# A block-sparse attention and mixture-of-experts kernel: three edits in how the attention copies, loads and scales

## The chip, the cores and the metric

The kernel runs on one core of one Trainium2 chip. The metric is the time of one execution on the device in microseconds (us). Engines are named as the profile names them: PE is TensorE (matrix products, and transposes as products with an identity), PEld its weight loads, DVE is VectorE, ACT is ScalarE, POOL is GpSimd, SP is SyncE, which here only issues transfers (DMAs). PSUM is the memory in banks into which PE writes its results.

## What is computed

Attention over 4 batches, 8 heads, 768 positions, 64 columns, with a mask by blocks of 32 positions; then every row of the result goes through two of eight experts.

```python
mask = np.abs(blk_i - blk_j) <= window                     # window = 1
mask = mask | (blk_i == 0) | (blk_j == 0) | (blk_i == n_blocks - 1) | (blk_j == n_blocks - 1)
for qb in range(n_blocks):
    for kb in sampled_blocks[qb]:                          # 3 blocks, drawn at random
        mask[qb * block:(qb + 1) * block, kb * block:(kb + 1) * block] = True
...
out = softmax(scale * q @ k.T where mask) @ v              # x, 3072 rows of 512
noisy = x @ w_gate + log1p(exp(x @ w_noise)) * noise       # the best two of 8 experts
out[row] = sum over its two experts e of weight[row, e] * relu(x[row] @ w1[e]) @ w2[e]
```

(The last three lines put a longer passage into short words; F, the hidden width, is 1024.)

## The kernel before

The attention comes first (0 to about 312 us of the profile), the experts after it. Only the attention is touched.

**Items.** A batch has six tiles t of 128 query rows, that is four blocks of 32, and each tile is worked in two head halves f: twelve items ("q", b, t, f). Four items more ("g", b, i, par) do the first and last block, which attend to everything. `steps` (L467) walks through all items as a pipeline. In step k it does, in this order of code: `turn` of item k (transpose its exponentials), `high` and `low` of item k-2 (its finished rows split into two fp16 parts, ACT L416 and POOL L423), `scores` of item k+2 (PE, L264), `soft` of it (DVE maximum L301, ACT exponentials L304), `cut` (DVE L346, zeroes a corner of the first and last tile), `global_av` (PE L382) and `av` of item k-1 (PE L359, with `norm` on DVE L366 to L369), and then the loads and preparations for later. Each engine runs its own instructions in that order and waits at semaphores for the others; the scores, the transposes and thus three steps share a ring of three PSUM tiles `ps` of two banks each.

**turn.** Eight transposes go into the two banks of the item's `ps`. DVE copies bank 0 out (L335, or L321 for g items) and ACT copies bank 1 (L333, L319) into `ptr` or `pgt`, from where `av` reads. `apart(it, bank, x)` declares that x doesn't depend on instructions that were noted for the other bank; the framework, which tracks a tile as a whole, then places no wait between the two. In the kernel before it is used for the transposes, not for ACT's copy.

**Rows of v.** A tile needs for each of its four blocks (three in the first and last tile) the three neighbouring blocks of v and three sampled ones. The neighbours lie ready in an array `vw`, 96 partitions by one block (j) by 2 KB; the sampled ("listed") rows are 64 KB transfers of their own (L232). `prefetch_v(b, t, half)` is called for half 0 in one step and for half 1 in the next; each call loads the neighbours of the half's two blocks (L227, 384 KB) and its six listed transfers. A tile has a buffer pair va, vb out of three; in the last batch out of two, so that a load there waits for the `av` of two tiles earlier.

**SP's queue.** SP issues the transfers one after another, in program order: v, `q` of a tile (L195), a piece of the next batch's keys `kk` (L172), stores, and from the last batch on the experts' weights `wraw` (L905) and zeroes for the output (L1334). An instruction issues only when the transfer eight before it has landed: the semaphores DMAHW0 to DMAHW7 take turns.

**Keys.** The next batch's keys come in six pieces of 256 KB, one an item, and `scale_k` (L184) multiplies a piece by 0.125 on POOL, i = 2t + f - 1 counting the items. `prefetch_k` (L204, L205 on POOL, L207 on ACT) then gathers a tile's keys out of `kk` into `kc`, which the scores read.

Of the kernel before, what the change touches and what calls it, by code (L numbers as in the profile page):

```python
# [16 lines left out]
AF = mybir.ActivationFunctionType  # L17
# [31 lines left out]
class Attention:  # L49
# [159 lines left out]
    def prefetch_v(self, b, t, half):  # L209
        nc, HD, J = self.nc, self.HD, self.NJ  # L210
        i = self.which(b, t)
        if half == 0:
            self.listed_rows[i] = []
        va, vb = self.va[i], self.vb[i]
        self.st["v", b, t] = va, vb
        js = self.real(t)
        first = t * J + js[0]
        if half == 0:
            self.unlisted = self.held_v.get(t)
            if self.unlisted is None:  # L220
                self.unlisted = self.numbers(self.mi[0:1, 3 * first:3 * (first + len(js))], mybir.EngineType.SP,
                                             self.NB * self.RB)
                if t in KEEP:
                    self.held_v[t] = self.unlisted
        js = [j for j in js if j // 2 == half]
        part = lambda x: x.rearrange("p (j c) -> p j c", j=J)[:, js[0]:js[-1] + 1]
        nc.sync.dma_start(va[0:96, js[0]:js[-1] + 1, 0:HD], part(self.vw[b, t]))  # L227
        rows = self.vx[b].rearrange("s c -> (s c)").bitcast(U8)
        for j in js:
            for n, d in enumerate((va[96:128, j], vb[0:32, j], vb[32:64, j])):  # L230
                at = self.unlisted[3 * (t * J + j - first) + n]
                x = nc.sync.dma_start(d[:, 0:HD].bitcast(U8), rows[bass.ds(at, self.RB)].rearrange("(p c) -> p c", p=32))  # L232
                self.listed_rows.setdefault(i, []).append(x)
                self.beside(x, self.weights.get(i, ()))
# [72 lines left out]
    def turn(self, it):  # L307
        nc = self.nc
        s = self.st.pop((it, "s"))
        if it[0] == "g":  # L310
            pg = self.st.pop((it, "p"))
            d = self.pgt[2 * it[2] + it[3]]
            for x in range(2):
                t = s[:, x].rearrange("p (c k) -> p c k", c=4)
                for c in range(4):
                    k = 96 * (4 * x + c)
                    self.apart(it, x, nc.tensor.transpose(t[0:96, c], pg[:, k:k + 96], self.ident))
                if x:
                    nc.scalar.activation(d[0:96, 4:8], t[0:96], AF.Copy)  # L319
                else:  # L320
                    read = nc.vector.tensor_copy(d[0:96, 0:4], t[0:96])  # L321
                    self.st[it, "read"].append((0, read))
            del self.st[it, "read"]
            return
        p = self.st.pop((it, "p"))
        d = self.st[it, "pt"] = self.pp.tile([P, 2, 2, 2, P], F32, name="ptr")
        for par in range(2):
            t = s[:, par].rearrange("p (e c k) -> p e c k", e=2, c=2)
            for e in (1, 0):
                for c in range(2):  # L330
                    self.apart(it, par, nc.tensor.transpose(t[:, e, c], p[:, 2 * e + par, P * c:P * c + P], self.ident))  # L331
            if par:
                nc.scalar.activation(d[:, par], t, AF.Copy)  # L333
            else:
                self.st[it, "read"].append((0, nc.vector.tensor_copy(d[:, par], t)))  # L335
        del self.st[it, "read"]
# [130 lines left out]
    def steps(self, router, done, background):  # L467
# [8 lines left out]
        for k in range(-2, n + 7):  # L476
# [48 lines left out]
            if new[0] == "q" and new[1] + 1 < B:  # L525
# [3 lines left out]
                if i == 2:  # L529
                    self.load_g(new[1] + 1)  # L530
                    self.load_ends(new[1] + 1)
                if 3 <= i <= 8:
                    self.scale_k(new[1] + 1, i - 3, 6, nc.gpsimd)
            if new[0] == "q" and new[3] == 1 and nk < len(tg):
                self.prefetch_k(*tg[nk])
                nk += 1
# [1041 lines left out]
```

## Time and profile before

| | |
|---|---|
| three runs | 857.63, 859.27, 862.04 us; median 859.27 us |
| profiled execution | 864.39 us, of which the span of the profile is 862.5 us |
| PE busy in the span | 792.3 us (92%) |
| DVE, ACT, POOL busy | 585.3, 401.4, 379.7 us |
| attention | 0 to about 312 us; last batch's part from about 236 us |
| experts | from about 320 us, PE busy throughout |

A row of a timeline shows the start, the duration, the engine, the line, the operation, what it writes and reads, how many instructions stand in the row, and in brackets how long the engine was idle just before and whose work ended that. "SPq" rows are issues by SP, several of them in one row with the short gaps between. The chain of waits follows the work that ended last back from the end; there a DMA row lasts from the issue to the landing that something waited for. "issue" is time for which the profile shows no reason.

### The profile page before, as it was taken

Reading aid. Unit: us, or ns where it says so; the run is one execution under the profiler, and the core shown is the slowest. Engines: PE = TensorE matmul, PEld = TensorE weight load, DVE = VectorE, ACT = ScalarE, POOL = GpSimd, SP = SyncE. Lnnn points to the kernel's source line nnn. Section 1 sums busy time; section 2 is a strip of 40 time slices with the busy share of each in tenths; the row PEclk is TensorE's granted clock in tenths of the full one; section 3 lists DMA queues with packets and bytes.
Section 4 is the critical chain, followed back from the end, with each engine's and each line's share of the span. In section 5 each row is a group of like instructions: output and inputs, shape, how many; then the busy total and the mean of one; then the engine's idle time right before and its main releaser. Section 6 shows DMA issues by size and latency. Waiting matters only on the chain.

```text
span 862.5 us, 24909 instructions
## 1 busy us (share of the span) xinstructions
PE 792.3 (92%) x9799; PEld 487.7 (57%) x9799; DVE 585.3 (68%) x1160; ACT 401.4 (47%) x736; POOL 379.7 (44%) x656
## 2 busy tenths in 40 slices
PE   7898889888877769999998999999999999999995
PEld 4676566565645647566586554554554554554552
DVE  6665697788787427762429698697697796796621
ACT  5868758848735325322113551542642633543500
POOL 5773587567554230130624526426335345323211
PEclk7999999999988859999999999999999999999998
DMA  7755786686669975650877839639539549533301
GB/s 229 218 177 169 213 233 187 199 242 188 226 189 266 224 178 162 192 186 22 219 161 140 241 110 235 189 101 234 172 112 230 170 128 216 164 98 104 97 31 50
DMA packets 119842, 148.87 MB, mean 173 GB/s; under 512 B 69515, under 2 KB 76300, under 8 KB 119714
## 3 DMA queue, kind: packets, MB, share of 16 engines
q1 hardware_dynamic: 107490, 109.22, 47.6%
q0 software_dynamic: 12224, 37.96, 14.0%
q8 instruction: 79, 1.29, 0.7%
q14 instruction: 49, 0.40, 0.2%
HBM read 107.28 MB, written 26.15 MB: 155 GB/s over the span
## 4 chain that ended last, share of the span: by engine, by line
PE 71%; DVE 11%; DMA 7%; ACT 5%; issue 3%; SPq 2%; POOL 1%; DVEq 0%; POOLq 0%; ACTq 0%
PE pc L1142 28%; PE pa L1095 11%; PE pd L1095 5%; PE po L359 5%; PE ps L264 4%; PE pa L1056 4%; PE pc L1095 3%; PE ps L331 3%; PE pd L1056 2%; PE pc L1151 2%; DMA va<-in_vx_dram 2%; DVE m L301 2%; DMA vb<-in_vx_dram 2%; DMA va<-in_vw_dram 2%; ACT p L304 2%
## 5 line engine op out<-in xcount | busy, mean ns | idle before, releaser
L1142 PE MATMUL pc<-w,hh 128*128 128x512 f16 x768 | 228.4, 379 | 0.0
L1175 POOL DMA_INDIRECT out_dram<-y,r_xT x46 | 64.2, 1395 | 220.3 <-DVE y L1174 181.6
L1142 PE MATMUL pc<-w,hl 128*128 128x512 f16 x384 | 145.5, 379 | 0.0
L1095 PEld LDWEIGHTS <-w 128*128 128x128 f16 x1008 | 99.2, 98 | 81.0 <-issue 6.2
L1142 PEld LDWEIGHTS <-hh 128*128 128x128 f16 x768 | 74.6, 98 | 86.4
L304 ACT ACTIVATE p<-ps,m 128x256 f32<-128x256 f32 x192 | 75.3, 476 | 24.6 <-DVE m L301 20.3
L204 POOL COPY kc<-kk 128x128 f32 x264 | 69.4, 300 | 23.0 <-PE ps L264 15.3
L359 PE MATMUL po<-va,ptr 128*32 128x68 f32 x1536 | 61.4, 236 | 17.2 <-DMA va<-in_vx_dram 10.2
L301 DVE TENSOR_REDUCE m<-ps 128x4 f32<-128x1024 f32 x48 | 58.6, 1221 | 22.6 <-PE ps L264 22.6
L998 POOL DMA_INDIRECT xg<-x_rows,r_xT x46 | 60.0, 1304 | 14.7 <-issue 14.7
L264 PE MATMUL ps<-kc,q 64*32 64x256 f32 x1536 | 57.0, 395 | 8.8 <-issue 3.8
L944 DVE SCALAR_TENSOR_TENSOR w<-wraw,w 128x1024 f16<-128x1024 f32 (+1 forms) x58 | 64.2, 1109 | 0.8 <-ACT w L940 0.8
L359 PE MATMUL po<-vb,ptr 128*32 128x68 f32 x1536 | 58.9, 233 | 4.8 <-issue 3.6
L1142 PEld LDWEIGHTS <-hl 128*128 128x128 f16 x384 | 37.6, 98 | 45.3
L1016 POOL DMA_INDIRECT pv<-out_dram,r_xT x44 | 49.0, 1113 | 28.2 <-issue 24.0
L1095 PE MATMUL pa<-tb,w 128*128 128x408 f16 x288 | 56.5, 340 | 3.3 <-ACT ta L1083 3.3
L359 PEld LDWEIGHTS po<-va,ptr 128*32 128x32 f32 x1536 | 42.8, 115 | 28.7 <-issue 8.4
L940 ACT ACTIVATE w<-wraw 128x1024 f16<-128x1024 f32 (+1 forms) x58 | 55.6, 959 | 6.6 <-DMA wraw<-in_moe_w_dram 6.6
L1174 DVE SCALAR_TENSOR_TENSOR y<-pc,r_xT,pv 128x512 f32<-128x512 f32 x37 | 27.7, 749 | 43.6 <-PE pc L1142 43.0
L1095 PE MATMUL pd<-tb,w 128*128 128x408 f16 x288 | 56.5, 336 | 0.0
L333 ACT ACTIVATE ptr<-ps 128x512 f32<-128x512 f32 x48 | 28.8, 600 | 57.6 <-DVE ptr L335 49.3
L1064 ACT ACTIVATE hh<-pa 128x408 f16<-128x408 f32 (+2 forms) x56 | 24.1, 443 | 65.6 <-PE pa L1056 53.2
(239 smaller groups left out, 1573.2 us busy)
## 6 DMA issues: line engine op xcount, KB each, us to landing
wraw<-in_moe_w_dram SPq DMA_DIRECT2D x64, 512.0 KB
va<-in_vw_dram SPq DMA_DIRECT2D x40, 384.0 KB
vb<-in_vx_dram SPq DMA_DIRECT2D x176, 64.0 KB
q<-in_qt_dram SPq DMA_DIRECT2D x24, 256.0 KB
va<-in_vx_dram SPq DMA_DIRECT2D x88, 64.0 KB
kk<-in_kt_dram SPq DMA_DIRECT2D x18, 256.0 KB
x_rows<-x SPq DMA_DIRECT2D x16, 256.0 KB
out_dram<-x SPq DMA_DIRECT2D x4, 768.0 KB
```

The lines of the kernel that those rows point to most:

```text
L204: nc.gpsimd.tensor_copy(kc[:, j, :, 3 + n], flat[:, bass.ds(self.listed(blk, n), P)].rearrange("p (n c) -> p n c", c=32))
L264: mm = lambda o, l, r: nc.tensor.matmul(o, l, r, start=True, stop=True, skip_group_check=True)
L301: nc.vector.tensor_reduce(m, s.rearrange("p a (e c) -> p a e c", e=2), axis=AX.X, op=ALU.max, negate=True)
L304: i = nc.scalar.activation(p[:, 2 * e + par], s[:, par, 256 * e:256 * e + 256], AF.Exp, bias=m[:, par, e:e + 1])
L359: nc.tensor.matmul(o[32 * j:32 * j + 32, h], d[:, h % 2, h // 2, x, 32 * j:32 * j + 32], self.values(v[:, self.slot(t, j)], 4 * f + h), st ...
L940: self.nc.scalar.activation(hi, t, AF.Copy, scale=WS)
L944: self.nc.vector.scalar_tensor_tensor(lo, t, WS, hi, op0=ALU.mult, op1=ALU.subtract)
L998: nc.gpsimd.indirect_dma_start(out=self.xg[0:m, c + self.place(u)], out_offset=None, in_=self.x_dram[0:nr], in_offset=bass.IndirectOffsetO ...
L1056: nc.tensor.matmul(ph[:, 0:m], w[:, wt, slot, kb % 2 * P:kb % 2 * P + P], r["xt"][:, kb, a, o:o + m], start=i == 0, stop=i == last)
L1095: nc.tensor.matmul(o, w[:, wt, slot, s * P:s * P + P], mv(s, a), start=i == 0 and p in tail, stop=i == 5, skip_group_check=True)
L1142: nc.tensor.matmul(py, h[:, f, o], w(f)[:, x], start=i == 0, stop=i == last)
L1175: d = nc.gpsimd.indirect_dma_start(out=self.out, out_offset=bass.IndirectOffsetOnAxis(ap=r["ix"][0:m, c:c + 1], axis=0), in_=y[0:m], in_of ...
```

## The change

Three edits, all in the class `Attention`.

```diff
+        if half == 0:
+            part = lambda x: x.rearrange("p (j c) -> p j c", j=J)[:, js[0]:js[-1] + 1]
+            nc.sync.dma_start(va[0:96, js[0]:js[-1] + 1, 0:HD], part(self.vw[b, t]))
         js = [j for j in js if j // 2 == half]
-        part = lambda x: x.rearrange("p (j c) -> p j c", j=J)[:, js[0]:js[-1] + 1]
-        nc.sync.dma_start(va[0:96, js[0]:js[-1] + 1, 0:HD], part(self.vw[b, t]))
...
-                    nc.scalar.activation(d[0:96, 4:8], t[0:96], AF.Copy)
+                    self.apart(it, 1, nc.scalar.activation(d[0:96, 4:8], t[0:96], AF.Copy))
...
-                nc.scalar.activation(d[:, par], t, AF.Copy)
+                self.apart(it, 1, nc.scalar.activation(d[:, par], t, AF.Copy))
...
-                if 3 <= i <= 8:
-                    self.scale_k(new[1] + 1, i - 3, 6, nc.gpsimd)
+                for x in ((0,), (1, 2), (3,), (4, 5))[i - 5] if 5 <= i <= 8 else ():
+                    self.scale_k(new[1] + 1, x, 6, nc.gpsimd)
```

(In the diff above the last loop is the program's own text as far as `scale_k`, whose argument is x in both.) Edit A makes ACT's copies of bank 1 independent of DVE's copies of bank 0. Edit B loads all neighbours of a tile with half 0, in one transfer of 768 KB (576 KB for the first and last tile); half 1 has only listed rows left. Edit C leaves i = 3 and 4 without a scale and does pieces 0; 1 and 2; 3; 4 and 5 at i = 5, 6, 7, 8.

What stands in the engines' queues, before and after. Line numbers after are larger by one from L228 on. "waits" names the semaphores: an engine's, or DMAHWn for the landing of a transfer. First ACT, an ordinary q item in the first batch: `turn`'s copy, the first fp16 part, four exponentials. Before:

```order
L333 ACTIVATE ptr<-ps 128x512 [waits DVE_49,PE_49]
L416 ACTIVATE x_955<-xr 128x2x128 [waits DMAHW2_49]
L304 ACTIVATE p<-ps,m 128x256 [waits DVE_49,Activation_49]
L304 ACTIVATE p<-ps,m 128x256 x3
L257 ACTIVATE vb_99<-ends_108 64x2x512
```

After:

```order
L334 ACTIVATE ptr<-ps 128x512 [waits PE_49,Activation_49]
L417 ACTIVATE x_949<-xr 128x2x128 [waits DMAHW2_49,DVE_49]
L305 ACTIVATE p<-ps,m 128x256 [waits DVE_49,Activation_49]
L305 ACTIVATE p<-ps,m 128x256 x3
L258 ACTIVATE vb_99<-ends_108 64x2x512
```

The order is the same; the wait for DVE has gone from the copy to the instruction behind it. On PE, at an item of the same kind, the transposes and the next scores. Before:

```order
L331 MATMUL ps<-r_ident,p 128x128 [waits DVE_49,Activation_49]
L331 MATMUL ps<-r_ident,p 128x128 x3
L331 MATMUL ps<-r_ident,p 128x128 [waits Activation_49]
L331 MATMUL ps<-r_ident,p 128x128 x3
L264 MATMUL ps<-kc_105,q 32x256 [waits Activation_49]
L264 MATMUL ps<-kc_105,q 32x256 x15
```

After:

```order
L332 MATMUL ps<-r_ident,p 128x128 [waits DVE_49,Activation_49]
L332 MATMUL ps<-r_ident,p 128x128 x3
L332 MATMUL ps<-r_ident,p 128x128 [waits Activation_49]
L332 MATMUL ps<-r_ident,p 128x128 x3
L265 MATMUL ps<-kc_105,q 32x256 [waits DVE_49,Activation_49]
L265 MATMUL ps<-kc_105,q 32x256 x15
```

The scores now wait for both copies by name, where one wait stood for both. On SP, tile 2 of the last batch (the transfers issued from 248.72 us on in the profile), from its neighbours to the third listed transfer of half 1. Before:

```order
L227 DMA va_96<-in_vw_dram 96x2x512 [waits DMAHW6_49,PE_49]
L232 DMA va_96<-in_vx_dram 32x2048 [waits DMAHW7_49]
L232 DMA vb_99<-in_vx_dram 32x2048 [waits DMAHW0_49]
L232 DMA vb_99<-in_vx_dram 32x2048 [waits DMAHW1_49]
L232 DMA va_96<-in_vx_dram 32x2048 [waits DMAHW2_49]
L232 DMA vb_99<-in_vx_dram 32x2048 [waits DMAHW3_49]
L232 DMA vb_99<-in_vx_dram 32x2048 [waits DMAHW4_49]
L1334 DMA out_dram<-xg 768x1x256 [waits DMAHW5_49,Pool_49]
L905 DMA wraw<-in_moe_w_dram 128x1024 [waits DMAHW6_49,Activation_49]
L195 DMA q<-in_qt_dram 128x512 [waits DMAHW7_49]
L227 DMA va_96<-in_vw_dram 96x2x512 [waits DMAHW0_49]
L232 DMA va_96<-in_vx_dram 32x2048 [waits DMAHW1_49]
```

After:

```order
L227 DMA va_96<-in_vw_dram 96x4x512 [waits DMAHW2_49,PE_49]
L233 DMA va_96<-in_vx_dram 32x2048 [waits DMAHW3_49]
L233 DMA vb_99<-in_vx_dram 32x2048 [waits DMAHW4_49]
L233 DMA vb_99<-in_vx_dram 32x2048 [waits DMAHW5_49]
L233 DMA va_96<-in_vx_dram 32x2048 [waits DMAHW6_49]
L233 DMA vb_99<-in_vx_dram 32x2048 [waits DMAHW7_49]
L233 DMA vb_99<-in_vx_dram 32x2048 [waits DMAHW0_49]
L1335 DMA out_dram<-xg 768x1x256 [waits DMAHW1_49,Pool_49]
L906 DMA wraw<-in_moe_w_dram 128x1024 [waits DMAHW2_49,Activation_49]
L195 DMA q<-in_qt_dram 128x512 [waits DMAHW3_49]
L233 DMA va_96<-in_vx_dram 32x2048 [waits DMAHW4_49]
L233 DMA vb_99<-in_vx_dram 32x2048 [waits DMAHW5_49]
```

The first L227 has twice the bytes and the second is gone; in both, L905 waits for the landing of the first L227, eight issues earlier. In all SP has 24 issues fewer, one for each tile. On POOL, from the finished rows of one item to the next tile's gather, in the first batch. Before:

```order
L423 TENSOR_TENSOR xe<-xr,xe 128x2x128 [waits DVE_49,Activation_49]
L184 TENSOR_SCALAR kk_103<-kk_103 128x512 [waits DMAHW0_49] x2
L204 REGISTER_ALU
L204 ISA
L204 COPY kc_104<-kk_102 128x4x32 [waits PE_49,Pool_49]
```

After:

```order
L424 TENSOR_TENSOR xe<-xr,xe 128x2x128 [waits Activation_49]
L204 REGISTER_ALU
L204 ISA
L204 COPY kc_104<-kk_102 128x4x32 [waits PE_49,Pool_49]
L204 REGISTER_ALU x2
```

The two scales that stood ahead of the gather stand later, where two of them follow each other at i = 6 and i = 8.

## Rows read from the trace of the kernel before

**Rows 1.** Page, busy time and share of the span by engine.
```profile
PE 792.3 (92%) x9799; PEld 487.7 (57%) x9799; DVE 585.3 (68%) x1160; ACT 401.4 (47%) x736; POOL 379.7 (44%) x656
```
**Rows 2.** Stretches: us, each engine's busy time, granted clock, DMA share, GB/s.
```profile
100.00:120.00 20.00, 17.15 (x536) 13.24 (x529) 16.12 (x53) 10.82 (x29) 11.81 (x34) 1.00 0.81 227
...
240.00:260.00 20.00, 13.27 (x293) 9.32 (x277) 18.04 (x65) 7.03 (x18) 13.67 (x36) 0.83 0.57 170
260.00:280.00 20.00, 15.71 (x406) 12.15 (x408) 15.86 (x36) 10.80 (x25) 9.19 (x23) 0.85 0.90 268
280.00:300.00 20.00, 15.30 (x330) 11.63 (x325) 8.11 (x16) 7.47 (x16) 5.18 (x8) 0.81 0.99 232
```
**Rows 3.** Groups by line, ACT, 0 to 320 us: busy, mean ns, idle before by releaser.
```profile
L304 ACT ACTIVATE p<-ps,m 128x256 f32<-128x256 f32 x192 | 75.3, 476 | 24.6 <-DVE m L301 20.3 <-DVE rc L366 2.1 <-issue 2.0
L333 ACT ACTIVATE ptr<-ps 128x512 f32<-128x512 f32 x48 | 28.8, 600 | 57.6 <-DVE ptr L335 49.3 <-PE ps L331 4.2 <-PE po L359 4.0
```
**Rows 4.** The same of DVE: the maximum over a tile of scores.
```profile
L301 DVE TENSOR_REDUCE m<-ps 128x4 f32<-128x1024 f32 x48 | 58.6, 1221 | 22.6 <-PE ps L264 22.6
```
**Rows 5.** Timelines of one turn at 232 us and one at 272 us.
```profile
232.28 0.59 ACT L319 ACTIVATE pgt<-ps 96x512 f32<-96x512 f32 x1 [0.58 <-DVE pgt L321]
232.93 1.10 PE L264 MATMUL ps<-kc,q 64*32 64x256 f32 x32 [0.34 <-ACT pgt L319]
...
271.44 1.09 PE L331 MATMUL ps<-r_ident,p 128*128 128x128 f32 x8
...
272.64 0.60 ACT L333 ACTIVATE ptr<-ps 128x512 f32<-128x512 f32 x1 [2.70 <-DVE ptr L335]
...
273.29 1.10 PE L264 MATMUL ps<-kc,q 64*32 64x256 f32 x32 [0.76 <-ACT ptr L333]
```
**Rows 6.** Waits of PE, 0 to 320 us: total us, times, longest.
```profile
PE ps L264 <- ACT pgt L319: 2.2, 4, 1.0
PE ps L264 <- ACT ptr L333: 2.1, 3, 0.8
```
**Rows 7.** Chain of waits, 60 to 85 us: start, us, what.
```profile
69.64 0.42 SPq L227
...
84.07 0.05 issue
```
**Rows 8.** Timeline of SP, POOL and PE around 105 us.
```profile
102.00 2.27 SPq L172 DMA_DIRECT2D kk<-in_kt_dram  x2
...
104.37 0.46 SPq L195 DMA_DIRECT2D q<-in_qt_dram  x1
...
105.71 0.62 POOL L184 TENSOR_SCALAR kk<-kk 128x512 f32<-128x512 f32 x1 [4.44 <-DMA kk<-in_kt_dram]
...
107.44 0.88 PE L264 MATMUL ps<-kc,q 64*32 64x256 f32 x24 [1.29 <-POOL kk L184]
```
**Rows 9.** PE's timeline: a wait for v before the last batch.
```profile
73.72 0.31 PE L359 MATMUL po<-va,ptr 128*32 128x68 f32 x4 [0.63 <-DMA va<-in_vx_dram]
```
**Rows 10.** Chain of waits, last batch (a DMA from issue to landing).
```profile
248.72 3.89 DMA va<-in_vw_dram
...
255.08 6.64 DMA va<-in_vw_dram
...
271.60 7.04 DMA va<-in_vx_dram
...
281.54 8.78 DMA vb<-in_vx_dram
```
**Rows 11.** PE's timeline, last batch: its waits for v.
```profile
278.78 0.73 PE L359 MATMUL po<-va,ptr 128*32 128x68 f32 x3 [3.42 <-DMA va<-in_vx_dram]
...
294.74 0.86 PE L359 MATMUL po<-va,ptr 128*32 128x68 f32 x3 [3.40 <-DMA va<-in_vx_dram]
...
304.88 0.44 PE L359 MATMUL po<-va,ptr 128*32 128x68 f32 x4 [2.18 <-DMA va<-in_vx_dram]
```
**Rows 12.** A short stretch of the last batch, columns as in the second group.
```profile
268.00:270.00 2.00, 2.00 (x48) 1.30 (x47) 1.82 (x7) 1.71 (x5) 1.78 (x6) 1.00 0.52 147
```

## The prediction

> **What bounds the kernel now.** I read the busy times first: PE works 792.3 us of the span [rows 1], so the question for every edit is which of PE's idle times it removes. The stretches say where those are. In a stretch in the middle of the attention PE is busy for 17.15 of 20 us at the full clock; in the last batch it is busy for 13.27, 15.71 and 15.30 of 20 us, at a granted clock of 0.81 to 0.85, with the DMA engines at 0.90 and 0.99 from 260 us on [rows 2]. Then I read who ends PE's idle time, stretch by stretch. Before the last batch the gaps are short, and many have no reason that the profile shows. In the last batch there are long ones, 3.42, 3.40 and 2.18 us, all ended by listed rows of v [rows 11]. The experts are PE without a break and no edit touches them, so whatever the attention gains at its end the whole gains, and no more. The end of the attention moves the experts' first weights and rows along with it.
>
> **Edit A, ACT's copy without DVE's.** The groups make this look large: ACT is idle for 49.3 us before its copies of bank 1 with DVE's copy as releaser [rows 3]. It is not what it looks. After the copy ACT has the first fp16 part and then the exponentials, and for those it waits again, 20.3 us in all, for the maximum on DVE, which takes 1.221 us and stands behind DVE's copy in DVE's queue [rows 3, 4]. A copy that is done earlier lets ACT wait earlier for the same maximum. What is left is PE waiting for ACT's copy in order to write into the bank again: 2.2 us and 2.1 us in all the attention [rows 6]. Of these seven waits I looked at ACT's row just before each. In five ACT was busy with work of its own, so the wait for DVE was not what held it. Two remain [rows 5]. At 232.28 ACT had been idle for 0.58 us for DVE, and PE then for 0.34 us: gain 0.34. At 272.64 ACT's 2.70 us of idle time seem a lot, but PE's own transposes ran from 271.44 for 1.09 us, to 272.53, and the copy can't start before them; it gains 272.64 - 272.53 = 0.11 us of the 0.76. The sum is -0.45 us. The bounds: 0, if the next wait takes it all, and -4.3 us, all of the two rows of PE's waits, which would need ACT's own work to go as well.
>
> What A adds is waits by name. PE's scores, which waited for ACT's copy alone and had DVE's in it, now wait for both, and the first fp16 part on ACT and the zeroing on DVE get one each. Counted over the order there are 38 waits more on PE beyond one an instruction. The trace before doesn't show their price on PE. The nearest row is a break of 0.05 us in a run of PE's products at a semaphore that had long been met [rows 7]: 38 x 0.05 = 1.9 us if PE does nothing beside them, 0 if they hide behind the product before. PE idles for about 14% in the middle stretch and the queue runs ahead of it, so I take a fifth: +0.4 us. Queued behind the new wait on ACT are the exponentials, which want a later result of DVE anyhow, so that nobody is delayed there.
>
> **Edit C, the scales two items later.** POOL waited 4.44 us for a piece of keys ahead of its gather at 105.71, and the profile then blames the scale for 1.29 us of PE's idle time [rows 8]. In the queue those two scales stand later now, so this wait of POOL goes. Does PE get its 1.29 us? The scores at 107.44 need three things: gathered keys, which POOL had finished before those scales; a free bank; and their q. That q was issued at 104.37 only, behind the two pieces of keys that took SP 2.27 us [rows 8], so 107.44 is 3.07 us after q's issue, and I hold q for the true releaser. C moves no load. So C is worth 0. Its bounds are -1.29 us (the profile's releaser is right) and +1.2 us: at i = 8 two scales of 0.62 us [rows 8] stand one after another ahead of the gather for the next batch's first tile, and each of three batches could pay for one of them, if the cover (ACT's and PE's work on the tile before) were gone, of which I allow two thirds.
>
> **Edit B, the neighbours in one transfer.** It takes 24 issues out of SP's queue, each about 0.42 us [rows 7], and puts the listed rows of half 1 that much closer to their front. Where a listed row ended PE's idle time, up to 0.42 us are gained. At 73.72 PE waited 0.63 us for one [rows 9]: -0.42. At 107.44 the q that PE waited for stands in the same queue behind a half's neighbours: another -0.42 of the 1.29 [rows 8]. Bounds for these: 0 (a transfer just as late for its bytes) and -1.92.
>
> In the last batch there is more to weigh. For: the last listed rows, awaited for 2.18 us at 304.88 [rows 11], stand one issue closer, -0.42; and in the two us from 268 the DMA engines were busy for 0.52 only [rows 12], while a half's neighbours waited in the queue behind q and stood to be issued at about 271. With B they are in flight by then and fill up to 2 x 0.48 = 0.96 us, of which the waits behind get the benefit: -1.0. Against: an issue waits for the landing of the transfer eight before. The 384 KB issued at 248.72 landed 3.89 us later, and its landing is what let SP go on [rows 10]. With twice the bytes it lands later, by at most 384 KB at the 268 GB/s of the busiest full stretch [rows 2]: 393 KB / 268 = 1.47 us. The experts' weights, a q and then half 1 of the listed rows are queued behind it. On the other side the second wait of this kind, 6.64 us for the half at 255.08 [rows 10], has lost its transfer, and in its place stands a smaller one. I take half of the 1.47 us as lost, +0.7, so that the last batch gives -0.42 - 1.0 + 0.7 = -0.7 us. B in all: -0.84 - 0.7 = -1.5 us.
>
> **Sum.** -0.45 + 0.4 + 0 - 1.5 = about -1.6 us. Against the profiled execution of 864.39 us that is 862.8 us; that execution is 5.1 us above the median of the runs shown, so for the median I take the same difference: 859.27 - 1.6 = 857.7 us.
>
> **Rivals.** First, **the last batch opens up**. Its long waits are 3.42 + 3.40 + 2.18 = 9.0 us [rows 11]. If neighbours in flight earlier halve them, that is -4.5 us, and PE then works nearer to the full clock: about 31 us of busy time at 0.81 to 0.85 [rows 2] carry some 5 us of slowness, of which half would be -2.5. With -1.0 from the rest: -8, 851 us. For it speaks that the listed rows end all three waits; against it that the DMA engines are at 0.99 from 280 on, and that B moves not one byte less. The Trainium skill has a rule on this side ("DMA: Bandwidth & Descriptors", Rules for kernel authors: coalesce many small transfers into a large one, since the fixed part dominates); what the rows show of a 384 KB transfer here is a landing in 3.89 us at best, so that the fixed part can't be read off them.
>
> Second, **the large transfer blocks the queue**, which ends slower. If all of the 1.47 us is lost at each of the four tiles that the last batch loads under full DMA engines, that is +5.9 us, less the 1.3 us that A and the early part of B give: +4.6, 863.9 us. The place is the ninth issue after each tile's first transfer. It decides from the point where 768 KB land later than SP needs for seven more issues, 7 x 0.42 = 2.9 us, and the 3.89 us of 384 KB are beyond that already [rows 10]; what speaks against it is that PE's first long wait for v comes only at 278.78 [rows 11], so that a queue that is late at 253 has time to catch up. By the fixed part and rate in the Trainium skill ("DMA: Bandwidth & Descriptors", Anatomy of one DMA, a fit for another path of issue: 2.0 us and 436 KB per us) a transfer of 768 KB would land in an estimated 3.8 us and one of 384 KB in 2.9 us; by that the ninth issue would be 0.9 us late and this rival's price 3.6 in place of 5.9.
>
> Third, **nothing moves**: the maximum on DVE and the DMA engines' bytes set every step, so that each gain is waited away at the next: 859.3 us. Here A has not made anything independent that matters, since the wait for DVE has only changed its place, from the copy to the instruction behind it. Fourth, **the scale did hold PE** at 107.44: C then gives up to -1.29 beside A and B, 856.4 us.
>
> **How the numbers follow.** The forecast, 857.7, gets 0.30; the last batch opening up 0.25; the blocked queue 0.20; nothing moves 0.15; the scale 0.10. A measurement of this kernel can tell about 0.5% from no change, that is 4.3 us: 855.0 to 863.6. Faster by more come nearly all of the first rival and some of the forecast's low side, 0.31; slower by more most of the second rival and a little beside it, 0.20; within it 0.49. The range goes from a little below the first rival, 850, to a little beyond the second, 865; the bounds of A's added waits and of C's double scales lie inside it.
>
> **What would show it.** A is right if ACT's idle time before its copies falls by tens of us, with that before the exponentials up by nearly as much, and PE's two rows of waits for ACT's copies little changed. C is right if POOL no longer waits for keys before the gather at about 105 us, while PE's scores there still wait, with q as the reason; wrong if that gap is gone. B is right if the waits of 0.63 and 2.18 us are shorter by about 0.4 us, and the gap in the DMA engines' work near 268 us is closed. The second rival shows as longer rows from issue to landing for the neighbours, with SP waiting on them; the first as a granted clock of 0.9 or more from 260 to 300 us. The forecast is wrong if attention ends more than 4 us away from where it does now.

## The result: slower, by edit B

The changed kernel takes 872.95 us in the median of 6 runs (866.19 to 880.64), the kernel before beside it 860.45 us. The ratio is 1.0115, 95% interval 1.0069 to 1.0161; the slowest of the six, 880.64 us, is left out of it as an execution in a slower state. A second set of six gave 1.0142 (1.0104 to 1.0179). So it is 10 to 12 us slower where 1.6 us of gain were forecast. The first profile of the changed kernel happened to catch that slowest execution; the lines below are from a profile of the second set, an execution of 871.13 us, close to that set's median of 871.08 us. Its first line of the page, busy time by engine:

```profile
PE 795.9 (92%) x9799; PEld 489.5 (56%) x9799; DVE 582.7 (67%) x1160; ACT 400.6 (46%) x736; POOL 378.7 (44%) x656
```

PE works through the same 9799 products as in [rows 1] and is busy 3.6 us longer, in a span of 869.3 us in place of 862.5. The experts' first product tells in which half the 6.8 us lie. In the timeline of PE it is, before and after:

```profile
319.86 0.43 PE L1056 MATMUL pa<-xta,w1s 128*128 128x320 f16 x1 [1.17 <-ACT r_xT L434]
```

```profile
326.96 0.43 PE L1057 MATMUL pa<-xta,w1s 128*128 128x320 f16 x1 [1.17 <-ACT r_xT L435]
```

It starts 7.1 us later, which is the whole difference. To place it inside the attention a landmark is of use: the router's small product `r_O`, which stands three times in this part of the trace. In PE's timeline, before:

```profile
120.33 0.18 PE L728 MATMUL po<-r_O,r_tri 128*128 128x48 f16 x1 [0.83 <-DVE og L388]
...
191.07 0.18 PE L728 MATMUL po<-r_O,r_tri 128*128 128x48 f16 x1 [0.83 <-DVE og L388]
...
247.20 0.20 PE L728 MATMUL po<-r_O,r_tri 128*128 128x48 f16 x1 [3.72 <-DVE r_O L715]
```

and after:

```profile
125.28 0.20 PE L729 MATMUL po<-r_O,r_tri 128*128 128x48 f16 x1
...
199.08 0.18 PE L729 MATMUL po<-r_O,r_tri 128*128 128x48 f16 x1
...
258.88 0.18 PE L729 MATMUL po<-r_O,r_tri 128*128 128x48 f16 x1 [2.91 <-DVE r_O L716]
```

The changed kernel is 5.0 us late at the first, 8.0 at the second, 11.7 at the third, and 7.1 at the end. These are single executions: A and C without B, which is not slower (below), passes the three landmarks at 124.21, 193.53 and 248.91 us and is thus 3.9, 2.5 and 1.7 us late; B alone passes them at 128.34, 203.54 and 262.56 us. The loss is made before the third landmark, in the batches that the prediction held to be safe.

Half of the 11.7 us are not waits. Up to the third landmark, before and after (us, each engine's busy time, granted clock, DMA share, GB/s):

```profile
0.00:247.20 247.20, 211.66 (x5065) 149.36 (x5066) 180.74 (x461) 175.95 (x372) 159.13 (x447) 0.98 0.70 205
```

```profile
0.00:258.88 258.88, 217.60 (x5065) 154.17 (x5066) 177.98 (x461) 176.21 (x374) 157.12 (x447) 0.94 0.72 196
```

PE is busy 5.9 us longer with the same 5065 products, at a granted clock of 0.94 in place of 0.98 (mean over the stretch), and idle 5.7 us longer. With B alone the busy time to this landmark is 216.4 us at 0.96, with A and C without B 212.4 us at 0.97. The profiles show that the slower products go with the longer gaps; that the gaps bring the clock down was not tested.

From the third landmark to the experts the changed kernel takes 68.1 us, the kernel before 72.7 us. That can't be put down to B: A alone takes 69.6 us there, A and C without B 69.4, C alone 72.3, B alone 69.7. The stretches of [rows 2] read now:

```profile
260.00:280.00 20.00, 16.95 (x396) 12.47 (x394) 19.31 (x50) 8.37 (x21) 11.67 (x30) 0.83 0.88 254
280.00:300.00 20.00, 14.82 (x360) 10.76 (x352) 12.01 (x28) 10.22 (x23) 7.99 (x14) 0.87 1.00 278
300.00:320.00 20.00, 13.69 (x360) 10.80 (x342) 6.34 (x17) 5.64 (x12) 4.13 (x7) 0.88 0.99 218
```

From 260 to 300 us the DMA engines are as full as before (0.88 and 1.00 against 0.90 and 0.99), and PE's clock is 0.83 and 0.87 where it was 0.85 and 0.81.

Where SP's queue loses time stands in its waits, 0 to 340 us (us in total, times, longest). Before, its waits at the listed rows for neighbours were:

```profile
SPq L232 <- DMA va<-in_vw_dram: 4.7, 6, 1.8
```

After:

```profile
SPq L233 <- DMA va<-in_vw_dram: 43.9, 20, 4.2
SPq L906 <- DMA va<-in_vw_dram: 4.4, 2, 2.7
SPq L615 <- DMA va<-in_vw_dram: 3.1, 1, 3.1
```

Twenty times, for 24 tiles, SP stands still at a listed row until the neighbours have landed, for 2.2 us on average; 19 of the twenty lie before the third landmark. SP's timeline shows one tile, the last of its batch, whose neighbours are 576 KB:

```profile
66.40 0.35 SPq L227 DMA_DIRECT2D va<-in_vw_dram  x1
66.85 0.41 SPq L233 DMA_DIRECT2D va<-in_vx_dram  x1
67.42 0.79 SPq L233 DMA_DIRECT2D vb<-in_vx_dram  x2
68.31 0.37 SPq L233 DMA_DIRECT2D va<-in_vx_dram  x1
68.84 0.78 SPq L233 DMA_DIRECT2D vb<-in_vx_dram  x2
69.71 0.37 SPq L233 DMA_DIRECT2D va<-in_vx_dram  x1
72.59 0.78 SPq L233 DMA_DIRECT2D vb<-in_vx_dram  x2
73.47 0.37 SPq L195 DMA_DIRECT2D q<-in_qt_dram  x1
```

One issue follows the other until eight are out, at 70.08. The ninth, the second listed row of half 1, waits until 72.59, 6.2 us after the neighbours were issued. Before, at the tile in the same place of the program:

```profile
64.28 0.35 SPq L227 DMA_DIRECT2D va<-in_vw_dram  x1
...
65.29 2.89 SPq L232 DMA_DIRECT2D vb<-in_vx_dram  x2
...
69.64 0.42 SPq L227 DMA_DIRECT2D va<-in_vw_dram  x1
...
72.81 0.37 SPq L195 DMA_DIRECT2D q<-in_qt_dram  x1
```

There SP had stood still too, inside an issue (two of them took 2.89 us), which no list of waits shows. So the 43.9 us are not all lost: over the first 18 tiles, from the start of a tile's first listed row to the end of its last, SP's timeline has 8.5 us on average in place of 7.5. The list of transfers gives the time from issue to landing, over those transfers whose landing it could tell, about half of them (KB each, median us):

```profile
va<-in_vw_dram SPq DMA_DIRECT2D x16, 768.0 KB, 7.4
vb<-in_vx_dram SPq DMA_DIRECT2D x176, 64.0 KB, 3.8
q<-in_qt_dram SPq DMA_DIRECT2D x24, 256.0 KB, 4.0
va<-in_vx_dram SPq DMA_DIRECT2D x88, 64.0 KB, 5.5
```

The page of the kernel before has no such times. But a trace holds the updates of the semaphores, and the last one for a transfer ahead of the semaphore's next transfer is its landing. By that the neighbours landed 4.6 us after their issue before and 6.5 us now (medians; most have 384 KB and 768 KB), and the listed rows of half 0, which stand right behind them, 4.0 us before and 5.7 us now. Those of half 1, which now have no neighbours of their own ahead, took 3.4 us before and 2.9 now.

And PE pays in several places. One of them is the place of [rows 8], where POOL has no scale any more ahead of its gather. The timeline of SP and PE:

```profile
107.64 0.37 SPq L195 DMA_DIRECT2D q<-in_qt_dram  x1
...
111.81 1.54 PE L265 MATMUL ps<-kc,q 64*32 64x256 f32 x24 [3.98 <-DMA q<-in_qt_dram]
```

The scores wait 3.98 us for q, where 1.29 us stood before, since q's issue was at 107.64 and not at 104.37: two tiles of neighbours have held SP up on the way. Others are put down to "issue", 14.5 us at L360 (5.4 us before), the products with v; what the profile puts down to listed rows there fell from 11.4 to 4.8 us, so that these three rows of waits go from 16.8 to 19.3 us.

### The profile page after: what moved, and what is told of

It is laid out like the page before. It is cut to its first block, busy times and chain, and to the rows that moved or that the text cites. A ratio compares the mean times of both kernels' runs of the same rounds, so it can differ in the third digit from the quotient of the medians.

```text
span 878.8 us, 24879 instructions
## 1 busy us (share of the span) xinstructions
PE 796.8 (91%) x9799; PEld 490.5 (56%) x9799; DVE 583.9 (66%) x1160; ACT 401.0 (46%) x736; POOL 380.6 (43%) x656
## 3 DMA queue, kind: packets, MB, share of 16 engines
q8 instruction: 79, 1.29, 0.6%
## 4 chain that ended last, share of the span: by engine, by line
PE 65%; DMA 11%; DVE 9%; ACT 6%; issue 4%; SPq 3%; POOL 1%; POOLq 0%; DVEq 0%; ACTq 0%
PE pc L1143 27%; PE pa L1096 10%; DMA va<-in_vw_dram 7%; PE pd L1096 5%; PE ps L265 4%; PE pa L1057 4%; PE po L360 3%; PE pc L1096 3%; PE pd L1057 2%; PE ps L332 2%; PE pc L1152 2%; SPq L233 2%; ACT p L305 2%; DVE m L302 1%; DMA vb<-in_vx_dram 1%
## 5 line engine op out<-in xcount | busy, mean ns | idle before, releaser
L265 PE MATMUL ps<-kc,q 64*32 64x256 f32 x1536 | 59.5, 415 | 15.4 <-DMA q<-in_qt_dram 4.2
L360 PE MATMUL po<-va,ptr 128*32 128x68 f32 x1536 | 59.5, 234 | 14.6 <-DMA va<-in_vx_dram 6.9
L360 PE MATMUL po<-vb,ptr 128*32 128x68 f32 x1536 | 58.2, 231 | 15.7 <-issue 12.2
L332 PE MATMUL ps<-r_ident,p 128*128 128x128 f32 x384 | 56.8, 294 | 0.0
L360 PEld LDWEIGHTS po<-vb,ptr 128*32 128x32 f32 x1536 | 44.2, 115 | 18.8 <-issue 15.8
L360 PEld LDWEIGHTS po<-va,ptr 128*32 128x32 f32 x1536 | 40.7, 114 | 24.0 <-DMA va<-in_vx_dram 8.7
```

Source lines behind the costliest of these rows:

```text
L265: mm = lambda o, l, r: nc.tensor.matmul(o, l, r, start=True, stop=True, skip_group_check=True)
L360: nc.tensor.matmul(o[32 * j:32 * j + 32, h], d[:, h % 2, h // 2, x, 32 * j:32 * j + 32], self.values(v[:, self.slot(t, j)], 4 * f + h), st ...
```

## The experiments

Each ratio is to the kernel before on the same chip, with its 95% interval.

**B alone.** Only the first hunk of the change:

```diff
+        if half == 0:
+            part = lambda x: x.rearrange("p (j c) -> p j c", j=J)[:, js[0]:js[-1] + 1]
+            nc.sync.dma_start(va[0:96, js[0]:js[-1] + 1, 0:HD], part(self.vw[b, t]))
         js = [j for j in js if j // 2 == half]
-        part = lambda x: x.rearrange("p (j c) -> p j c", j=J)[:, js[0]:js[-1] + 1]
-        nc.sync.dma_start(va[0:96, js[0]:js[-1] + 1, 0:HD], part(self.vw[b, t]))
```

> Edit B alone, the copies and the scales as before. If the slowdown is the queue's (a 768 KB transfer lands 7.1 us after its issue in the trace of the changed kernel, SP waited 46.1 us for such landings, 4.7 before), B alone is as slow as all three: ratio 1.010 to 1.016, SP's wait at the listed rows again above 40 us. If the slowdown comes from the waits that A has moved or from the two scales in a row of C, B alone stays within 0.4% of before.

Measured: 1.0155 (1.0115 to 1.0194), 875.91 us. SP's wait at the listed rows is there again:

```profile
SPq L233 <- DMA va<-in_vw_dram: 43.8, 20, 6.0
```

B alone is the slowdown.

**A and C without B.** The first hunk undone, the three others left:

```diff
-        if half == 0:
-            part = lambda x: x.rearrange("p (j c) -> p j c", j=J)[:, js[0]:js[-1] + 1]
-            nc.sync.dma_start(va[0:96, js[0]:js[-1] + 1, 0:HD], part(self.vw[b, t]))
         js = [j for j in js if j // 2 == half]
+        part = lambda x: x.rearrange("p (j c) -> p j c", j=J)[:, js[0]:js[-1] + 1]
+        nc.sync.dma_start(va[0:96, js[0]:js[-1] + 1, 0:HD], part(self.vw[b, t]))
```

> Edits A and C without B. By the queue theory nothing is left of the slowdown: ratio 0.996 to 1.002, attention's end within 2 us of before. If A or C slows (PE waiting for a gather, 1.9 and 3.9 us for POOL in the changed kernel's trace), the ratio is 1.005 or more and those two waits of PE stay.

Measured: 0.9967 (0.9933 to 1.0001), 860.40 us. Nothing of the slowdown is left.

**C alone.** Against the kernel before:

```diff
-                if 3 <= i <= 8:
-                    self.scale_k(new[1] + 1, i - 3, 6, nc.gpsimd)
+                for x in ((0,), (1, 2), (3,), (4, 5))[i - 5] if 5 <= i <= 8 else ():
+                    self.scale_k(new[1] + 1, x, 6, nc.gpsimd)
```

> Edit C alone. Forecast 0 with bounds of -1.3 and +1.2 us: ratio 0.998 to 1.002. PE's 1.29 us wait before the scores near 107 us stays if q is its releaser and goes if the scale is. The rival, that PE now waits for gathers that stand behind two scales, gives +2 us or more, ratio above 1.002.

Measured: 1.0034 (1.0001 to 1.0067), just above the range of the forecast. In this profile PE lost 2.50 us at 44.51 in one gap that the profile puts down to "issue"; A and C together show one of 2.92 us at nearly the same place and are yet not slower, and a later kernel with C (the second half early with A and C) has one of 0.71 us there, like the kernel before (0.67 us). The other sign that was named for this side, PE waiting for gathers, is one wait of 0.8 us. At the place of [rows 8] the scores (106.92 us) don't wait at all in this profile: their q was issued at 100.07, early enough, so that the case of a late q without the scales is not in it. I take C as no measurable change, and its small excess here as not explained.

**A alone.** Against the kernel before:

```diff
-                    nc.scalar.activation(d[0:96, 4:8], t[0:96], AF.Copy)
+                    self.apart(it, 1, nc.scalar.activation(d[0:96, 4:8], t[0:96], AF.Copy))
...
-                nc.scalar.activation(d[:, par], t, AF.Copy)
+                self.apart(it, 1, nc.scalar.activation(d[:, par], t, AF.Copy))
```

> Edit A alone. Forecast -0.45 us with bounds of 0 and -4.3, plus 0.4 us for waits: ratio 0.997 to 1.001. ACT's idle time before its copies with DVE as releaser goes from 49.3 us to near 0, and the time before the exponentials up by most of it. If A and C together (0.9967) owe their gain to A, the ratio is 0.992 to 0.997.

Measured: 0.9992 (0.9965 to 1.0019). ACT's groups, 0 to 320 us, against [rows 3]:

```profile
L304 ACT ACTIVATE p<-ps,m 128x256 f32<-128x256 f32 x192 | 75.1, 476 | 57.0 <-DVE m L301 48.3 <-DVE rc L366 4.2 <-DVE r_hi L747 3.0
L333 ACT ACTIVATE ptr<-ps 128x512 f32<-128x512 f32 x48 | 29.0, 604 | 15.2 <-PE ps L331 14.8
```

The 49.3 us of waiting for DVE's copy are gone, 14.8 us of them are now a wait for PE's transposes, and the wait for the maximum has grown from 20.3 to 48.3 us. In both groups together 82.2 us of idle time have become 72.2: nearly the same idle time under another name.

**Neighbours at half 0 in two transfers.** B, but with two transfers of 384 KB, one right behind the other:

```diff
         if half == 0:
-            nc.sync.dma_start(va[0:96, js[0]:js[-1] + 1, 0:HD], part(self.vw[b, t]))
+            for h in range(2):
+                q = [j for j in js if j // 2 == h]
+                nc.sync.dma_start(va[0:96, q[0]:q[-1] + 1, 0:HD], part(self.vw[b, t], q))
```

> Neighbours of a tile all issued at half 0 as in B, but as two transfers of 384 KB, with A and C undone: the same bytes at the same place in SP's queue, one issue more. If it is the size of a single transfer that holds a slot of the eight too long, SP's waits for neighbours fall well below 46 us and the ratio is 1.000 to 1.005. If it is the place (768 KB of neighbours ahead of every listed row), it is as slow as B alone: within 0.3% of it.

Measured: 1.0113 (1.0070 to 1.0156), 872.86 us; SP's waits at the listed rows fall to 18.8 us:

```profile
SPq L235 <- DMA va<-in_vw_dram: 18.8, 21, 1.9
```

So neither answer alone: SP waits less than half as long, and yet the time is at most a little better. Nor does the time follow SP's standing still alone.

**The neighbours of half 1 left out.** B's queue, issue for issue, with half of the bytes: from the fourth tile on the one transfer carries only half 0's blocks, and half 1's are not loaded.

```diff
         if half == 0:
-            nc.sync.dma_start(va[0:96, js[0]:js[-1] + 1, 0:HD], part(self.vw[b, t]))
+            some = js if b * self.T + t < 3 else [j for j in js if j < 2]
+            nc.sync.dma_start(va[0:96, some[0]:some[-1] + 1, 0:HD], part(self.vw[b, t]))
```

> SP's queue exactly as in edit B alone, one transfer of neighbours a tile at half 0, but from the fourth tile on it carries only the two blocks of half 0 (384 KB in place of 768 KB); the neighbours of half 1 are not loaded, so that part of the computation uses old rows. If B's price is the bytes at that place, the slowdown is gone and the 24 missing issues show: ratio 0.985 to 1.000, SP's waits for neighbours from 52.5 back to 10 to 20 us. If it is something else in the queue's order (the semaphores that now take turns otherwise), it stays at 1.010 or more.

Measured: 0.9905 (0.9873 to 0.9938), 854.93 us. SP's waits for neighbours are 18.1 us in all (52.5 with B alone). It is not the queue's order; the same queue is fast with 384 KB there. Part of the gain against before is that the kernel moves some 7 MB less in all (17 tiles by 384 KB and 4 by 192 KB), so it says nothing of what 24 issues are worth.

**The merged transfer on POOL's queue.** It takes none of the eight places of SP. Against B:

```diff
-            nc.sync.dma_start(va[0:96, js[0]:js[-1] + 1, 0:HD], part(self.vw[b, t]))
+            nc.gpsimd.dma_start(va[0:96, js[0]:js[-1] + 1, 0:HD], part(self.vw[b, t]))
```

> Edit B, with the 768 KB transfer issued by POOL, so that it takes none of the eight transfers that SP may have in flight; same bytes, same step of the program, A and C undone. By the slot theory (SP stands still until the large transfer has landed) the slowdown is gone: ratio 0.990 to 1.003, SP's waits for landings at or below the 21.5 us of before. By the rival (the listed rows come later because 384 KB more of neighbours share the DMA engines with them) it stays: 1.010 or more. POOL pays for the issues; in the last batch POOL waits for the buffer where SP did.

Measured: 1.0084 (1.0057 to 1.0111), 870.95 us. SP now waits for no neighbours, but 21.9 us for listed rows, 16 times:

```profile
SPq L233 <- DMA va<-in_vx_dram: 11.5, 7, 2.9
SPq L233 <- DMA vb<-in_vx_dram: 10.4, 9, 3.0
```

About half of B's price stays without any slot held. Whether that half is POOL's own cost the next run had to tell.

**The two halves of before on POOL's queue.** Against the kernel before:

```diff
-        nc.sync.dma_start(va[0:96, js[0]:js[-1] + 1, 0:HD], part(self.vw[b, t]))
+        nc.gpsimd.dma_start(va[0:96, js[0]:js[-1] + 1, 0:HD], part(self.vw[b, t]))
```

> The kernel before with its two transfers of 384 KB a tile issued by POOL, at the places of before. Neither this nor the merged transfer on POOL (1.0084) holds a slot of SP's eight, so the difference of the two is what merging costs without slots. If the slot is the whole price of B, this one is as slow as the merged one on POOL: 1.006 to 1.011 (all of it POOL's own cost). If sharing the DMA engines is the price, it is 1.000 or below.

Measured: 0.9984 (0.9957 to 1.0012), 859.95 us. POOL's issues cost nothing that can be measured, so merging costs about 1.0084 - 0.9984 = 1.0% even where SP holds no slot for it (each ratio is to the kernel before on its own chip; the two chips differ). SP's waits for listed rows in this one:

```profile
SPq L232 <- DMA vb<-in_vx_dram: 7.2, 10, 1.9
SPq L232 <- DMA va<-in_vx_dram: 3.5, 5, 1.7
```

10.7 us where the merged one has 21.9. By the semaphores' updates the listed rows of half 1 land later with the merged transfer (median 4.8 us after their issue against 3.8), those of half 0 don't (4.0 against 4.3), and the neighbours themselves take 7.0 us against 5.5. So the 1.0% can come from listed rows that share the DMA engines with 768 KB, or from half 0's products, which now wait for a transfer that carries half 1's blocks too; no run separates these.

**The second half early, but behind the rows.** Both halves' neighbours at half 0, as two transfers of 384 KB, the second behind half 0's six listed rows:

```diff
+        late = [j for j in js if j // 2 == 1]
         js = [j for j in js if j // 2 == half]
-        nc.sync.dma_start(va[0:96, js[0]:js[-1] + 1, 0:HD], part(self.vw[b, t]))
+        if half == 0:
+            nc.sync.dma_start(va[0:96, js[0]:js[-1] + 1, 0:HD], part(self.vw[b, t], js))
...
                 self.beside(x, self.weights.get(i, ()))
+        if half == 0:
+            nc.sync.dma_start(va[0:96, late[0]:late[-1] + 1, 0:HD], part(self.vw[b, t], late))
```

> The neighbours of half 1 are loaded with half 0, as in B, but as a second transfer of 384 KB behind the six listed rows. The bytes are as early as with two transfers at half 0 (1.0113), but no listed row of half 0 stands behind them. If the place ahead of the listed rows is what costs, 0.998 to 1.004; if any 384 KB more at half 0 cost, 1.005 to 1.012.

Measured: 0.9979 (0.9949 to 1.0010), 861.99 us. The bytes are as early as in B within one step, and the price is gone. Against the two transfers at half 0 (1.0113) only the place of the second one is different: what cost there was the place ahead of the listed rows.

**The merged transfer behind the rows**, 768 KB behind half 0's six (`real` holds all blocks of the tile):

```diff
                 self.beside(x, self.weights.get(i, ()))
+        if half == 0:
+            nc.sync.dma_start(va[0:96, real[0]:real[-1] + 1, 0:HD], part(self.vw[b, t]))
```

> Edit B with the 768 KB transfer behind the six listed rows of half 0 in place of ahead of them. Slot theory: the slot is held just as long, but the ninth issue after it now lies in the next step, after a pause of SP: half or more of B's 1.55% is gone, ratio 1.002 to 1.008, SP's waits between 21 and 45 us. If the bytes matter, half 0's rows are early and half 1's as late as in B: 1.010 or more.

Measured: 1.0058 (1.0038 to 1.0077), 871.36 us. Better than B, worse than 384 KB ahead and 384 KB behind (0.9979). The time is where the slot theory put it, but half 0's neighbours have also moved behind the rows, and that alone costs as much (1.0076, under "Neighbours always behind the rows"); so this run doesn't show a price of the slot. SP now stands still in the next step, at the keys and stores:

```profile
SPq L172 <- DMA va<-in_vw_dram: 11.4, 5, 3.4
SPq L638 <- DMA va<-in_vw_dram: 9.7, 6, 2.0
SPq L231 <- DMA va<-in_vw_dram: 6.5, 5, 2.0
```

**The merged transfer one step later**, with half 1. Against B:

```diff
-        if half == 0:
+        if half == 1:
             part = lambda x: x.rearrange("p (j c) -> p j c", j=J)[:, js[0]:js[-1] + 1]
```

> All 768 KB of a tile in one transfer, issued one step later, with half 1 and ahead of its listed rows. Half 0's rows then have nothing ahead of them. Slot theory: as slow as B, 1.010 to 1.016, since the slot is held as long. If lateness of the last listed rows decides, slower than B, 1.015 to 1.030, since the bytes come one step later too. Below 1.008 would mean that half 0's rows are the ones that matter.

Measured: 1.0059 (1.0030 to 1.0088), 869.28 us: neither as slow as B, as the slot alone would have it, nor slower. Half 0's rows, free of the neighbours, are early (median landing 2.5 us after their issue against 5.7 with B alone), and half 1's late (5.5 against 2.8). A ratio below 1.008 was to mean that half 0's rows are the ones that matter, and the run speaks for that. SP's waits have moved to q and the keys (13.4 us at q, 5.9 at the keys).

**Neighbours always behind the rows.** The kernel before, each half's 384 KB behind its six rows:

```diff
-        nc.sync.dma_start(va[0:96, js[0]:js[-1] + 1, 0:HD], part(self.vw[b, t]))
...
                 self.beside(x, self.weights.get(i, ()))
+        nc.sync.dma_start(va[0:96, js[0]:js[-1] + 1, 0:HD], part(self.vw[b, t]))
```

> The kernel before, two transfers of 384 KB a tile, each behind the six listed rows of its half in place of ahead of them. If PE's waits for listed rows (11.4 us before, of DMA) come from the neighbours ahead of them, they shrink and the ratio is 0.993 to 0.999. If what lands last simply changes its name, 0.999 to 1.004.

Measured: 1.0076 (1.0048 to 1.0105), 870.30 us. A miss of both expectations: slower, though SP waits for neighbours only 6.1 us in all. The neighbours are then the last of a half to be issued, and a product needs them as much as the rows. By the semaphores' updates a half's data are complete later: for half 0 on average 7.6 us after the tile's first issue, 6.6 us before; for half 1 11.8 against 10.4 us (first 18 tiles). That this is what PE waits for was not tested.

**Four pieces.** The kernel before with one transfer of 192 KB for each block:

```diff
-        nc.sync.dma_start(va[0:96, js[0]:js[-1] + 1, 0:HD], part(self.vw[b, t]))
+        for j in js:
+            nc.sync.dma_start(va[0:96, j, 0:HD], part(self.vw[b, t], j))
```

> The other direction: a half's neighbours as two transfers of 192 KB (four a tile, 48 issues more in all than B, 24 more than before), at the place of before. If a transfer's size holds the slot, SP's waits fall below the 21.5 us of before and the ratio is 0.995 to 1.001; if the number of issues is what costs (0.4 us each on SP), 1.001 to 1.006.

Measured: 1.0078 (1.0053 to 1.0103), 871.47 us. SP's waits for neighbours fall, to 8.9 us in all from 11.9, and the kernel is slower, more than either expectation had it. The count in the expectation is wrong: the list of transfers has 88 of 192 KB where the kernel before has 48 transfers, so that there are 40 issues more than before and 64 more than in B. I put the price down to these issues; no run separates it from the smaller transfers.

**The second half early with A and C.** The best place of the neighbours (the diff under "The second half early") with the two harmless edits (those under "A alone" and "C alone").

> The second half's neighbours behind half 0's listed rows (0.9979 alone) with edits A and C (0.9967 alone). If the two add, 0.992 to 0.997; if both gained the same idle time or both were noise, 0.997 to 1.001.

Measured: 0.9950 (0.9924 to 0.9976), 856.55 us: a version faster than both kernels, by about half a per cent against before. How much of it is the neighbours' and how much A's and C's, the runs can't tell, since each alone has an interval that holds 1.

**The whole change again**, with no edit.

> The changed kernel once more, for a ratio on the same chip as these. 1.010 to 1.016, as B alone and the first measurement; clearly below B alone (1.0155) only if A and C bring something beside B.

Measured: 1.0142 (1.0104 to 1.0179). It lies beside B alone; A and C neither save nor spoil it.

## Why the prediction was wrong, step by step

**Bounds of the kernel.** Right that PE is nearly full, that whatever the attention gains or loses at its end the whole gains or loses (7.1 us there, 6.8 us of span) and that the experts don't take part. Wrong in what followed from it, that the stretch with the largest gaps is the stretch to watch. The loss came where the gaps were small, and half of it as slower products, which the prediction counted for one rival alone.

**Edit A.** Right in mechanism: idle time that only changed its name, from the copy to the exponentials. Its size, -0.45 us and +0.4 us for added waits, is below what the runs can tell (0.9992, 0.9965 to 1.0019). PE's two rows of waits for ACT's copies are 4.0 and 1.3 us with A alone, 2.2 and 2.1 before.

**Edit C.** Probably right that q, and not the scale, released PE at 107.44. In the trace before, the last update of q's semaphore is at 107.30, 0.14 us ahead of the scores; the second of the two scales ended at 107.33, so that the times alone can't tell the two apart, but the scores don't read what it wrote. In the changed kernel, with the scales gone from there, PE waits 3.98 us, and the profile itself names q; but there B had made q late. C alone came out 0.3% up, A and C 0.3% down; about zero is what is left.

**Edit B before the last batch.** This is the step that failed: "Where a listed row ended PE's idle time, up to 0.42 us are gained", with bounds of 0 and -1.92 us. The issue that is saved was priced, and no loss was allowed for. The wait for the transfer eight before was priced for the last batch alone. In fact SP stood still at these rows 19 times before the third landmark, 39.7 us in all, and by the landmark the kernel was 11.7 us late after three batches, in this one execution. Two things were overlooked. With 384 KB SP waited at the listed rows 4.7 us in all, six times; with twice the bytes nearly every tile has its turn. And the bytes ahead of the rows are not free for the rows: those of half 0, which the prediction left as they were, landed 5.7 us after their issue in place of 4.0, where it looked for a gain at those of half 1.

**Edit B in the last batch.** -0.7 us were forecast, and no run shows them or refutes them. From the third landmark to the experts the changed kernel is 4.6 us shorter than the profile of the kernel before, but two kernels without B are also 3 us shorter (A alone, A and C), and that scatter is larger than the term. The wait that was priced at half of 1.47 us is there: in the last batch SP stood still for 4.2 us at a listed row and twice, 4.4 us in all, at the weights.

**The rivals.** The second, the large transfer that blocks the queue, is what the trace shows: SP is blocked at the place that it named (the ninth issue after a tile's first transfer) and by its point of decision (landing later than seven issues take, 2.9 us, against 7.4 us measured). It was given 0.20, four tiles in place of twenty, and 1.47 us a tile, where SP stood still 2.2 us. It is not the whole price, as two transfers (1.0113 with less than half of the waits at the rows) and POOL's queue (1.0084 with no slot held) show; that its 863.9 us come near what was measured is no proof of it. That PE's first long wait came only at 278.78 was taken as speaking against it; I read it now as a queue that is late every 10 us and has little time to catch up, which no run tested. The rule of the Trainium skill cited beside the first rival ("DMA: Bandwidth & Descriptors", Rules for kernel authors: coalesce small transfers) names transfers under 64 KB as those that pay mostly overhead; the ones that were merged here have 384 KB, so that the runs don't test it. The estimate worked out from the same page's Anatomy of one DMA, 3.8 us for 768 KB, is half of the 7.4 us measured with listed rows beside it; the fit is for POOL's path, and on POOL's queue the merged transfers landed after 7.0 us (median, by the semaphores).

**What stays open.** That the 768 KB ahead of half 0's rows make B slow is shown: half of the bytes there, or half of them behind the rows, and the price is gone (0.9905, 0.9979). How the price divides is not. The slot that SP holds has a price of its own by one comparison across chips (B alone 1.0155 against 1.0084 on POOL's queue); 1.0% stays between the two kernels on POOL's queue, by late rows or by late neighbours; and a queue moved to POOL also changes what SP issues when. Nor is it shown why the granted clock is lower. And what PE waits for with neighbours always behind the rows was not followed up.

## What to carry to other kernels

A queue that waits, as SP's here, for the landing of the transfer eight issues earlier is held by its slowest transfer: before merging two transfers, compare the landing time of the merged one with the time that the queue needs to issue the rest of its window, at every place where it is issued, and not only where waits already show. Put the bytes that nobody waits for yet behind the small ones that somebody does, and keep them in pieces that land within the window; here that turned +1.5% into no measurable loss (0.9979). But keep what the next products need ahead of the rows: each half's own neighbours behind its rows cost 0.8%. When a queue's waits have gone up, look also at how long the products take: here half of the time lost up to the third landmark was products at a lower granted clock. An idle time with a large total in front of one instruction is worth what is left after the next wait of the same engine, and this can be read off the next group's row before trying.

## What the runs showed of the hardware

Small transfers are not fast because they are small: in the changed kernel 64 KB of listed rows landed in 3.8 us (into vb) and 5.5 us (into va) in the median, 256 KB of q in 4.0 us and 768 KB in 7.4 us, in one and the same queue. An issue by SP can itself last long: most took about 0.4 us, but 46 of the 409 up to 330 us in the trace of the kernel before took over 1 us. Issuing the same bytes from POOL's queue in place of SP's cost POOL 31.4 us of issuing for 48 transfers and the kernel nothing that can be measured (0.9984). The same 5065 products of the attention kept PE busy 211.7 us at a mean granted clock of 0.98 and 217.6 us at 0.94.
